# Retention + SwiGLU kernel: the ramp written in a new order, with powers of the decay spread by TensorE, small operations moved to GpSimd, and loads issued at other places

## The chip, the cores and the metric

One core of a Trainium2 chip (trn2) runs the kernel. The metric is the time of one execution in microseconds (us), the median of the runs. TensorE (PE, with its weight loads PEld), VectorE (DVE), ScalarE (ACT), GpSimd (POOL) and SyncE (SP, which issues loads) each run their own instruction list in order and wait for one another by semaphores.

## What is computed

Decayed linear attention in blocks (4 sequences of 768, 8 heads of width 64), whose output goes row by row through an RMS norm and a gated feed-forward layer (512 to 1536 to 512):

```python
Dmask = np.where(rel >= 0, lam[:, None, None] ** rel[None, :, :], 0.0)
intra = np.einsum('bhic,bhjc->bhij', qb, kb) * Dmask[None]
intra = np.einsum('bhij,bhjd->bhid', intra, vb)
inter = np.einsum('bhid,bhde->bhie', qb * lam_pow[None], kv_state)
kv_state = lam_block[None, :, None, None] * kv_state + np.einsum('bhsd,bhse->bhde', kb_dec, vb)
...
xn = x / rms * rms_g
g = xn @ w_gate
silu = g * (1.0 / (1.0 + np.exp(-g)))
return (silu * (xn @ w_val) @ w_out)
```

## The kernel before

The 3072 rows are cut into six row blocks m of 512, the heads into four pairs p, the hidden width into twelve blocks f of 128. `Pair(m, p)` makes the attention of a row block and a pair, `Weights(f)` turns the raw weights of block f into f16 high and low parts, `Hidden(m, f)` makes the gate and value products (three parts each: high by high, low by high, high by low), `Norm(m)` the RMS norm. In the names of the ramp p03 is `Pair(0, 3)`, w2 is `Weights(2)`, h0 is `Hidden(0, 0)`, n0 is `Norm(0)`.

The first six units of row block 0, the attention of row blocks 0 and 1 and the weights of blocks 0 to 5 are issued by `ramp()`, one list of calls written out by hand. Nothing reorders them: each call puts its instructions at the end of the lists of its engines, and each engine works through its list in order. After the ramp `unit()` runs the remaining units, one after the other.

A Pair on TensorE: `scores` (tile pa, 8 products), `state_sums` (pst, 6 or 8 products of 64 columns), `mix_chunks` (po, 8 products), `mix_states` (po again, 6 products). On the other engines: `decay_k` on ScalarE, `decay_a` on VectorE (pa times the mask), `decay_q`, `states` on VectorE, `keep_output` and `keep_squares`. `row_sums` (pss, 4 products per pair), `mean`, `root` (y, on GpSimd), `spread` (pr) and `scaled` (xn), `high`, `low` make the normed rows that the gate products read, in four parts kk.

A Weights block: `lift` (ScalarE), `convert` (VectorE, two operations, whole or by parts), `square` (ScalarE), `norm` (pn, TensorE), `scale`, `high` (ScalarE), `low`, `undo`; its part for the output product has `lift_o`, `convert_o`, `high_o`, `low_o`.

The products share few banks: `pg` and `pv` hold one gate and one value product each, and in turn the state sums and the mixed output of pairs that are not `odd`; the next user waits until the last reader is done. The other banks are po0 to po3 and `ps`.

Loads: `load_next()` issues the next of a fixed list on the SP queue. Here q11 stands for the load of q, k and v of `Pair(1, 1)` (two pieces of 512 KB), g3 for the gate and value weights of block 3 (`raw_gv`, 1024 KB) and o3 for its output weights (`raw_o`, 512 KB). The list is q10, g1 with o0, g2 with o1, q11, g3, q12, g4, q13, g5 and so on; o2, o3 and later ones are issued at the end of `convert_o` of the block two below. A load into a buffer that is still read waits on SP, and what is behind it waits as well.

`busy(n)` issues n products whose result nobody reads.

Of the kernel before, what the change touches and what calls it, by code (L numbers as in the profile page):

```python
# [23 lines left out]
def retention_swiglu_kernel(  # L24
# [130 lines left out]
    def powers(p, part):  # L155
        if part < 2:
            h = 2 * p + part
            nc.vector.tensor_tensor_scan(
                mask[:, h, :], lam_b[:, h : h + 1].broadcast_to([P, P]), ident, 0.0,
                ALU.mult, ALU.add,  # L160
            )
        else:
            nc.vector.tensor_tensor_scan(
                pw[:, p, :], lam_p[:, p : p + 1].broadcast_to([P, P]), zeros, 1.0,
                ALU.mult, ALU.add,
            )
# [23 lines left out]
    def scales_of(pmax):  # L190
        nc.vector.tensor_reduce(gmax, pmax[:, :P], axis=mybir.AxisListType.X, op=ALU.max)
        nc.vector.tensor_single_scalar(ge, gmax.bitcast(I32), 0x7F800000, op=ALU.bitwise_and)
        nc.vector.tensor_scalar_min(ge, ge, float(252 * EXP))
        nc.vector.tensor_scalar(sx.bitcast(I32), ge, -1.0, float(253 * EXP), ALU.mult, ALU.add)
        nc.vector.tensor_scalar(gs, gcol, sx, XS, ALU.mult, ALU.mult)
        nc.vector.tensor_scalar_add(cx.bitcast(I32), ge, float(EXP))
        nc.vector.tensor_scalar_mul(cx, cx, 1.0 / (XS * WS))
# [15 lines left out]

    zeros = wg[:, NF - 1, 1].bitcast(F32)[:, :P]
    nc.scalar.mul(zeros, ones, 0.0)
# [142 lines left out]
    class Weights:  # L358
# [79 lines left out]
        def undo(self):  # L438
            inv = small.tile([P, 2], F32, tag="inv", name=f"inv_{self.f}")
            nc.vector.tensor_scalar_add(inv.bitcast(I32), self.e2, float(64 * EXP))  # L440
            nc.vector.tensor_scalar_mul(cg[:, self.f, :], inv, cx)
# [19 lines left out]
    class Pair:  # L461
# [48 lines left out]
        def states(self):  # L510
            m, p = self.m, self.p
            for c in range(GC):
# [4 lines left out]
                if g % SEQ_CH == 0:  # L517
                    nc.vector.tensor_copy(new, self.pst[:, c, :])
                else:
# [298 lines left out]
    def ramp():  # L818
# [5 lines left out]
        powers(0, 0)  # L824
        largest()
        powers(0, 1)
        powers(2, 0)
        busy(2, 3)
        powers(2, 1)
        busy(4)  # L830
        powers(1, 2)
        powers(3, 1)
        powers(1, 0)
        powers(1, 1)
        p00.decay_k()
# [72 lines left out]
        n0.spread()
        w0.scale()
        w1.convert(1)  # L910
        w0.high(0)
        w1.square(1)
        n0.scaled(0)
        n0.high(0)
        p10.state_sums()
        busy(2, 1)
# [3 lines left out]
        n0.scaled(1)  # L920
        w0.high(1)
        n0.high(1)
        p10.states()
        n0.scaled(2)
        n0.high(2)
        p10.mix_chunks()
        load_next()
        n0.scaled(3)
        busy(2, 3)
        n0.low(1, nc.vector)  # L930
        w0.low(0)
        n0.low(2, nc.vector)
        n0.high(3)
        n0.low(3, nc.vector)
        w0.lift_o()
        w1.high(0)
        w0.low(1)
        w0.undo()
        w1.low(0)
        busy(2, 3)  # L940
        w1.pn = ps_att.tile([P, 2, G], F32, tag="ps", name="pn_1")[:, 0]
        w1.norm(slice(1, 2))
        w1.scale(slice(1, 2))
        p10.decay_q(nc.gpsimd)
        p10.mix_states()
        p10.keep_output(nc.scalar)
        h0.gate(0)
        h0.val(0)
        h0.gate(1)
        n0.low(0, nc.gpsimd)  # L950
        h0.gate(2)
        h0.val(1)
        h0.val(2)
        w2.lift()
        h0.silu()
        w2.convert(part=0)
        h1.gate(0)
        w1.undo()
        h0.mul()
        h1.gate(1)  # L960
        w3.lift()
        w1.high(1)
        h1.gate(2)
        w2.convert(part=1)
        w1.low(1)
        w2.square(0)
        w2.square(1)
        h1.val(0)
        h1.val(1)
        w3.convert(part=0)  # L970
        w0.convert_o()
        p10.keep_squares()
        h1.silu()
        w2.pn = ps_att.tile([P, 2, G], F32, tag="ps", name="pn_2")[:, 0]
        w2.norm()
        load_next()
        w2.scale()
        w2.high(0)
        p11.decay_k()
        w2.high(1)  # L980
        h1.val(2)
        p11.scores()
        h2.gate(0)
        w3.convert(part=1)
        w2.low(0)
        high_o(0)
        w2.undo()
        h1.mul()
        h2.gate(1)
        w1.lift_o()  # L990
        w2.low(1)
        h2.gate(2)
        h2.val(0)
        h2.val(1)
        h2.val(2)
        w3.square(0)
        h0.high()
        w1.convert_o()
        h0.low()
        low_o(0, nc.vector)  # L1000
        h0.out(3)
        p11.decay_a()
        high_o(1)
        h2.silu()
        h2.mul()
        w3.square(1)
        load_next()
        p12.decay_k()
        h0.out(2)
        p11.decay_q(nc.vector)  # L1010
# [3 lines left out]
        w2.lift_o()  # L1014
        h1.high()
        p11.state_sums()
        p11.states()
        w2.convert_o()
        w3.high(1)
        w3.high(0)  # L1020
        p11.mix_chunks()
        w4.lift()
        load_next()
        w3.low(0)
        w3.low(1)
        p12.scores()
        p11.mix_states()
        h3.gate(0)
        high_o(2)
        w3.undo()  # L1030
        w4.convert(part=0)
        h3.gate(1)
        h0.out(0)
        h1.low()
        h3.gate(2)
        p12.decay_q(nc.vector)
        w4.convert(part=1)
        p11.keep_squares()
        p11.keep_output(nc.scalar)
        low_o(1, nc.gpsimd)  # L1040
        h3.val(0)
        h1.out(2)
        h3.val(1)
        p12.decay_a()
        w3.lift_o()
        h3.val(2)
        h3.silu()
        h0.out(1)
        w4.square(0)
        w4.square(1)  # L1050
        w4.pn = ps_att.tile([P, 2, G], F32, tag="ps", name="pn_4")[:, 0]
        w4.norm()
        p11.add_squares(nc.vector)
        h3.mul()
        w4.scale()
        p12.state_sums()
        p12.states()
        p12.mix_chunks()
        p12.mix_states()
        w4.high(1)  # L1060
        load_next()
        w4.high(0)
        w4.lift_o()
        low_o(2, nc.vector)
        w4.low(1)
        w4.low(0)
        p12.keep_output(nc.vector)
        p12.keep_squares()
        w5.lift()
        p13.scores()  # L1070
        h4.gate(0)
        h1.out(0)
        p13.decay_q(nc.gpsimd)
        h2.high()
        p13.decay_k()
        w3.convert_o()
        high_o(3)
        load_next()
        h4.gate(1)
        w5.convert(part=0)  # L1080
        h1.out(1)
        h4.gate(2)
        load_next()
        w4.undo()
        h2.low()
        w5.convert(part=1)
        w5.square(0)
        h4.silu()
        h4.val(0)
        h4.val(1)  # L1090
        h4.val(2)
        h1.out(3)
        h2.out(1)
        p13.decay_a()
        low_o(3, nc.vector)
        w5.square(1)
# [244 lines left out]
```

## Time and profile before

| | us |
|---|---|
| median of 3 runs | 676.25 (675.94 to 676.49) |
| the profiled execution, whole | 677.75 |
| its span, first to last instruction | 675.9 |
| TensorE busy in the span | 667.7 |

The profile is of one execution. Its span leaves out 1.85 us of the execution's own time (677.75 less 675.9). In the trace the ramp ends at 95.25 us, where the gate product of the first `unit()` starts.

### The profile page before, as it was taken

To read this page: it belongs to the slowest core of one execution; us is meant where nothing else is said; L and a number is where in the kernel's file an instruction comes from. 1 tells how busy PE (TensorE), PEld (TensorE's weight loads), DVE (VectorE), ACT (ScalarE), POOL (GpSimd) and SP (SyncE) were. 2 spreads that over 40 slices of the span, in tenths; PEclk is the share of its full clock that TensorE was granted. 3 is DMA by queue.
4 is the path that set the end of the run, shared out by engine and by line. 5 is a ranking of instruction groups with operands and counts; after the bars stand their busy time and mean duration, and the time that the engine had idled before them with its cause. 6 is when DMAs were issued, how large, how long until landed. Compare 5 with 4: busy or idle time off the path is not lost.

```text
span 675.9 us, 9923 instructions
## 1 busy us (share of the span) xinstructions
PE 667.7 (99%) x4156; PEld 359.1 (53%) x4156; DVE 323.1 (48%) x575; ACT 248.3 (37%) x438; POOL 78.8 (12%) x76
## 2 busy tenths in 40 slices
PE   8998999999999999999999999999999999999997
PEld 7856665555666444554444555444465444444443
DVE  7797857777545386332812322631341462211112
ACT  3785556776425435322213222221331221211111
POOL 2200130011214303230000111000011000000000
PEclk9999999999999999999999999999999999999999
DMA  8936622541014201122001022100100000100001
GB/s 320 365 120 225 233 109 97 185 156 63 1 64 171 79 0 63 64 99 89 1 0 58 29 102 79 47 0 1 63 1 1 1 0 1 63 0 1 1 0 62
DMA packets 14299, 50.96 MB, mean 75 GB/s; under 512 B 1712, under 2 KB 1968, under 8 KB 12848
## 3 DMA queue, kind: packets, MB, share of 16 engines
q1 hardware_dynamic: 13968, 49.69, 20.2%
q8 instruction: 32, 0.52, 0.3%
q10 hardware_dynamic: 288, 0.66, 0.3%
q14 instruction: 11, 0.09, 0.0%
HBM read 44.05 MB, written 6.29 MB: 74 GB/s over the span
## 4 chain that ended last, share of the span: by engine, by line
PE 95%; DMA 2%; DVE 2%; issue 0%; ACT 0%; DVEq 0%; SPq 0%
PE pv L697 27%; PE pg L697 27%; PE acc L716 10%; PE acc L718 9%; PE acc L717 9%; PE pa L476 4%; PE po L536 3%; PE po L547 3%; PE pst L505 2%; DMA raw_gv<-in_weights_dram 1%; PE pss L600 1%; DMA cs<-in_consts_dram 0%; DVE xn L675 0%; DVE w L233 0%; PE pss L647 0%
## 5 line engine op out<-in xcount | busy, mean ns | idle before, releaser
L697 PE MATMUL pv<-x,wv 128*128 128x512 f16 x864 | 199.1, 379 | 1.9 <-ACT x L567 1.9
L697 PE MATMUL pg<-x,wg 128*128 128x512 f16 x864 | 199.9, 379 | 0.2 <-ACT x L680 0.2
L789 DVE SCALAR_TENSOR_TENSOR sg<-pv,cv,sg 128x512 f32<-128x512 f32 x54 | 40.5, 750 | 241.7 <-PE pv L697 241.7
L697 PEld LDWEIGHTS <-wv 128*128 128x128 f16 x864 | 84.3, 98 | 102.7 <-issue 3.2
L697 PEld LDWEIGHTS <-wg 128*128 128x128 f16 x864 | 82.7, 98 | 101.2 <-issue 4.9
L718 PE MATMUL acc<-wo,hh 128*128 128x512 f16 (+1 forms) x288 | 110.3, 383 | 0.0
L717 PE MATMUL acc<-wo,hh 128*128 128x512 f16 (+1 forms) x288 | 110.2, 383 | 0.0
L782 ACT ACTIVATE sg<-pg,cg 128x512 f32<-128x512 f32 x72 | 49.3, 684 | 163.4 <-PE pg L697 163.3
L799 ACT CAST hh<-sg 128x512 f16<-128x512 f32 (+1 forms) x72 | 44.5, 617 | 162.1 <-DVE sg L789 158.3
L716 PE MATMUL acc<-wo,hh 128*128 128x512 f16 x216 | 82.0, 380 | 0.0
L496 POOL TENSOR_TENSOR qkv<-qkv,pw 128x512 f32<-128x512 f32 x22 | 28.2, 1285 | 239.7 <-PE pa L476 233.9
L806 DVE TENSOR_TENSOR hh<-sg,hh 128x512 f16<-128x512 f32 x54 | 38.0, 704 | 27.4 <-ACT hh L799 27.4
L716 PEld LDWEIGHTS <-hh 128*128 128x128 f16 x216 | 21.1, 98 | 26.6 <-issue 2.8
L718 PEld LDWEIGHTS <-hh 128*128 128x128 f16 x216 | 21.1, 98 | 25.5
L717 PEld LDWEIGHTS <-hh 128*128 128x128 f16 x216 | 21.2, 98 | 23.4
L716 PE MATMUL acc<-wo,hl 128*128 128x512 f32 x72 | 32.4, 450 | 0.0
L492 DVE TENSOR_TENSOR a<-pa,mask 128x1024 f32<-128x1024 f32 x24 | 29.3, 1222 | 5.9 <-PE pa L476 5.9
L476 PE MATMUL pa<-qkv 64*128 64x128 f32 x384 | 27.9, 285 | 0.0
L476 PEld LDWEIGHTS pa<-qkv 64*128 64x128 f32 x384 | 23.3, 187 | 8.3 <-issue 6.5
L536 PE MATMUL po<-a,qkv 128*64 128x128 f32 x384 | 25.7, 275 | 0.0
L486 ACT ACTIVATE qkv<-qkv,mask 128x256 f32<-128x256 f32 x48 | 21.7, 502 | 8.8 <-DMA qkv<-in_qkv_dram 8.8
L567 ACT COPY x<-po 128x512 f32<-128x512 f32 x22 | 12.8, 580 | 28.6 <-PE po L547 28.6
(131 smaller groups left out, 598.0 us busy)
## 6 DMA issues: line engine op xcount, KB each, us to landing
qkv<-in_qkv_dram SPq DMA_DIRECT2D x47, 512.0 KB, 4.8
raw_gv<-in_weights_dram SPq DMA_DIRECT2D x11, 1024.0 KB, 7.0
raw_o<-in_weights_dram SPq DMA_DIRECT2D x12, 512.0 KB, 3.8
out_dram<-o SPq DMA_DIRECT2D x23, 256.0 KB, 2.3
partial<-in_weights_dram SPq DMA_DIRECT2D x2, 512.0 KB, 12.3
qkv<-in_qkv_dram ACTq DMA_DIRECT2D x1, 512.0 KB, 4.1
out_dram<-o SPq DMA_DIRECT2D x1, 128.0 KB, 2.1
out_dram<-o ACTq DMA_DIRECT2D x1, 128.0 KB, 1.9
```

The costliest lines, as they stand in the source:

```text
L476: nc.tensor.matmul(self.pa[:, j, c, :], self.kT[r, c, :], self.qT[r, c, :], start=True, stop=True,)
L492: nc.vector.tensor_mul(self.a, self.pa, decay.broadcast_to([P, 2, GC, P]))
L496: eng.tensor_mul(self.qT, self.qT, pw[:, p : p + 1, :].broadcast_to([P, GC, P]))
L536: nc.tensor.matmul(po[r, c, :], self.v[:, c, r], self.a[:, j, c, :], start=c == 0, stop=False, skip_group_check=True,)
L697: nc.tensor.matmul(ps, w[:, kk, :], x[:, kk, :], start=i == kk == 0, stop=i == 2 and kk == NK - 1,)
L716: nc.tensor.matmul(acc, hl[:, ts_], oh, start=first, stop=False)
L717: nc.tensor.matmul(acc, hh[:, ts_], ol, start=False, stop=False)
L718: nc.tensor.matmul(acc, hh[:, ts_], oh, start=False, stop=last)
L782: nc.scalar.activation(self.sg, self.pg, AF.Silu, scale=cg[:, self.f, 0:1])
L789: nc.vector.scalar_tensor_tensor(out, self.pv, factor, self.sg, ALU.mult, ALU.mult)
L799: nc.scalar.copy(self.hh, self.sg)
L806: nc.vector.tensor_sub(self.hl, self.sg, hh)
```

## The change

- The powers of lam that multiply q (`pw`) were four scans on VectorE. Now the mask's first row is spread by two products a pair (`spread_powers`, tile pp in bank po3) and multiplied by lam on ScalarE (`powers_of`). The operation that made a tile of zeros for the scans is gone.
- `scales_of` is cut: the largest value is taken on VectorE early, the five small operations that follow run on GpSimd. `undo` runs on GpSimd for w0, w1, w3 and w5. `low_o` of blocks 0 to 3 is on GpSimd (before: block 1 alone of these), of blocks 4 and 5 on VectorE.
- The first state of a sequence (`first_state`) is a call of its own, on ScalarE for most pairs.
- One group of unread products is put in bank po0, that of the state sums: `busy(3, 0)`.
- The ramp's list is written in another order throughout. q10, g1 and g2, q11 are issued behind one `mix_states` each.

```diff
+    def powers(h):
+        nc.vector.tensor_tensor_scan(
+            mask[:, h, :], lam_b[:, h : h + 1].broadcast_to([P, P]), ident, 0.0,
+            ALU.mult, ALU.add,
+        )
+
+    def spread_powers(p):
+
+        ps = ps_out.tile([P, DM], F32, tag="po3", name=f"pp_{p}")
+        for j, r in enumerate(heads):
+            nc.tensor.matmul(
+                ps[r, :P], ident[:, 0:1].broadcast_to([P, D]), mask[:, 2 * p + j, :], start=True, stop=True
             )
...
+        return ps
+
+    def powers_of(p, ps):
+        nc.scalar.mul(pw[:, p, :], ps[:, :P], lam_p[:, p : p + 1])
...
+    def scales_of(eng):
+        eng.tensor_scalar_min(ge, ge, float(252 * EXP))
+        eng.tensor_scalar(sx.bitcast(I32), ge, -1.0, float(253 * EXP), ALU.mult, ALU.add)
+        eng.tensor_scalar(gs, gcol, sx, XS, ALU.mult, ALU.mult)
+        eng.tensor_scalar_add(cx.bitcast(I32), ge, float(EXP))
+        eng.tensor_scalar_mul(cx, cx, 1.0 / (XS * WS))
...
-    zeros = wg[:, NF - 1, 1].bitcast(F32)[:, :P]
-    nc.scalar.mul(zeros, ones, 0.0)
...
-        def undo(self):
+        def undo(self, eng=nc.vector):
             inv = small.tile([P, 2], F32, tag="inv", name=f"inv_{self.f}")
...
+        def first_state(self, eng=nc.vector):
             m, p = self.m, self.p
+            for c in range(GC):
+                g = m * GC + c
+                if g % SEQ_CH == 0:
+                    copy = nc.scalar.copy if eng is nc.scalar else eng.tensor_copy
+                    copy(state[:, p, g % SLOTS, :], self.pst[:, c, :])
```

The ramp's list around the first gate products and around the loads, as it stands now:

```python
row_sums(0, 3)
busy(2, 3)
w0.pn = ps_out.tile([P, DM], F32, tag="po3", name="pn_0")
w0.norm(slice(0, 1))
...
busy(3, 0)
w0.norm(slice(1, 2))
...
n0.spread()
w1.convert(0)
p10.scores()
w0.scale(slice(1, 2))
n0.scaled(3)
p10.state_sums()
w1.square(0)
n0.scaled(2)
...
n0.scaled(0)
...
n0.scaled(1)
n0.high(1)
p10.decay_a()
...
h0.gate(0)
n0.low(2, nc.gpsimd)
w0.high(1)
p10.mix_chunks()
w1.lift_o()
w0.lift_o()
p10.first_state(nc.scalar)
w1.lift(1)
...
w2.lift()
h0.val(0)
n0.low(1, nc.vector)
w1.high(0)
w2.convert(part=0)
h0.gate(1)
h0.gate(2)
h0.silu()
w1.convert(1)
load_next()
w2.convert(part=1)
load_next()
busy(4)
h1.gate(0)
...
h0.val(1)
...
w0.convert_o()
```

**TensorE around the first gate product (tile pg).** Before, all of `Pair(1, 0)` (pa, pst, then po twice) and four groups of unread products stand ahead of it (pn is the norm of w0 and w1, pr the norm's spread):

```order
L476 MATMUL pa_0_410<-qkv_0_267 128x128 x8
L146 MATMUL unread_421<-ident 128x128 x2
L412 MATMUL pn_424<-ssq_397,ones 128x2
L633 MATMUL pr_433<-ident,y_408 128x128 x4
L505 MATMUL pst_0_450<-qkv_0_267 64x64 x6
L146 MATMUL unread_457<-ident 128x128 x2
L412 MATMUL pn_424<-ssq_430,ones 128x1
L536 MATMUL po_0_475<-a_0_419,qkv_0_267 64x128 x8
L146 MATMUL unread_488<-ident 128x128 x2
L146 MATMUL unread_503<-ident 128x128 x2
L412 MATMUL pn_506<-ssq_430,ones 128x1
L547 MATMUL po_0_475<-qkv_0_267,state 64x128 x6
```

Now only pa and pst of `Pair(1, 0)` stand ahead of it, and po of `Pair(1, 0)` comes behind:

```order
L146 MATMUL unread_414<-ident 128x128 x2
L416 MATMUL pn_417<-ssq_395,ones 128x1
L146 MATMUL unread_423<-ident 128x128 x3
L416 MATMUL pn_417<-ssq_395,ones 128x1
L645 MATMUL pr_438<-ident,y_431 128x128 x4
L480 MATMUL pa_0_445<-qkv_0_273 128x128 x8
L509 MATMUL pst_0_458<-qkv_0_273 64x64 x6
L416 MATMUL pn_417<-ssq_465,ones 128x1
L709 LDWEIGHTS wg
L709 MATMUL pg_0_489<-x_276,wg 128x512
```

Both po rows of `Pair(1, 0)` moved behind the first gate product; of eight unread products five are left ahead of it, and four more now stand ahead of the first gate product of h1; pn of w0 is cut in two.

**SP, the loads from q11 on.** Before (q11, g3, o2, q12, o3, g4, o4):

```order
L86 DMA qkv_1_389<-in_qkv_dram 128x1024 x2
L101 DMA raw_gv_484<-in_weights_dram 128x2048
L109 DMA raw_o_590<-in_weights_dram 128x1024
L86 DMA qkv_2_598<-in_qkv_dram 128x1024 x2
L109 DMA raw_o_665<-in_weights_dram 128x1024
L101 DMA raw_gv_683<-in_weights_dram 128x2048
L109 DMA raw_o_713<-in_weights_dram 128x1024
```

Now (q11, g3, q12, o2, o3, g4, q13):

```order
L86 DMA qkv_1_388<-in_qkv_dram 128x1024 x2
L101 DMA raw_gv_534<-in_weights_dram 128x2048
L86 DMA qkv_2_537<-in_qkv_dram 128x1024 x2
L109 DMA raw_o_572<-in_weights_dram 128x1024
L109 DMA raw_o_638<-in_weights_dram 128x1024
L101 DMA raw_gv_642<-in_weights_dram 128x2048
L86 DMA qkv_3_670<-in_qkv_dram 128x1024 x2
```

o2 moved behind q12, and q13 ahead of o4.

**ScalarE around the silu of h2 (tile sg_2).** Before, o1 is lifted (L221, raw_o_387) ahead of it; w3 is lifted further up:

```order
L430 ACTIVATE wg<-w_546,sc_602 128x512
L486 ACTIVATE qkv_1_389<-qkv_1_389,mask 128x4x64 x2
L430 ACTIVATE wv<-w_546,sc_602 128x512
L249 CAST wo_629<-wg 128x512
L221 ACTIVATE wg<-raw_o_387 128x512
L408 ACTIVATE junk_0_659,ssq_658<-w_564 128x512
L799 CAST hh_0_661<-sg_0_548 128x512
L249 CAST wo_676<-wg 128x512
L782 ACTIVATE sg_2_678<-pg_2_622,cg 128x512
L408 ACTIVATE junk_1_681,ssq_658<-w_564 128x512
```

Now w3 is lifted (L225, w_628) and then o2 (L225, raw_o_572) ahead of it:

```order
L794 ACTIVATE sg_1_606<-pg_1_545,cg 128x512
L811 CAST hh_0_626<-sg_0_530 128x512
L225 ACTIVATE w_628<-raw_gv_534 128x1024
L225 ACTIVATE wg<-raw_o_572 128x512
L434 ACTIVATE wv<-w_512,sc_589 128x512
L794 ACTIVATE sg_2_634<-pg_2_612,cg 128x512
L253 CAST wo_644<-wg 128x512
L412 ACTIVATE junk_0_682,ssq_681<-w_628 128x512
L412 ACTIVATE junk_1_685,ssq_681<-w_628 128x512
```

The instruction that needs o2 moved ahead of the silu of h2 and of both squares of w3 (L412, junk).

## Rows read from the trace of the kernel before

**Rows 1.** The page, part 1: busy us, share of the span, instructions.

```profile
PE 667.7 (99%) x4156; PEld 359.1 (53%) x4156; DVE 323.1 (48%) x575; ACT 248.3 (37%) x438; POOL 78.8 (12%) x76
```

**Rows 2.** Windows by stage: busy time per engine, TensorE clock, DMA share, GB/s.

```profile
22.00:24.25 2.25, 2.25 (x21) 2.13 (x20) 0.79 (x2) 1.91 (x6) 0.00 (x0) 1.00 1.04 390
32.48:57.90 25.42, 25.23 (x171) 14.08 (x170) 21.94 (x46) 18.49 (x35) 1.61 (x1) 1.00 0.52 178
57.90:60.00 2.10, 0.19 (x2) 0.00 (x1) 1.50 (x3) 2.10 (x5) 0.00 (x0) 1.00 0.96 326
60.00:95.25 35.25, 35.25 (x239) 24.27 (x238) 27.35 (x49) 21.02 (x39) 8.33 (x7) 1.00 0.49 193
```

**Rows 3.** Timeline at 57.9 us: start, microseconds, engine, line; in brackets idle before.

```profile
47.97 0.43 SPq L101 DMA_DIRECT2D raw_gv<-in_weights_dram  x1
...
57.34 1.12 ACT L221 ACTIVATE w<-raw_gv 128x1024 f32<-128x1024 f32 x1 [4.16 <-DMA raw_gv<-in_weights_dram]
...
59.99 1.02 PE L697 MATMUL pv<-x,wv 128*128 128x512 f16 x4 [1.91 <-ACT x L567]
```

**Rows 4.** Timeline of TensorE in the ramp.

```profile
1.46 2.93 PE L146 MATMUL unread<-ident 128*128 128x128 f32 x12 [1.46 <-POOL one L210]
...
6.53 1.38 PE L146 MATMUL unread<-ident 128*128 128x128 f32 x10
...
9.55 1.09 PE L536 MATMUL po<-a,qkv 128*64 128x128 f32 x16
...
12.11 1.16 PE L476 MATMUL pa<-qkv 64*128 64x128 f32 x16
...
38.03 2.75 PE L697 MATMUL pg<-x,wg 128*128 128x512 f16 x12
```

**Rows 5.** Timeline of the norm of row block 0, in four engines.

```profile
24.36 0.16 DVE L620 TENSOR_SCALAR ms<-pss 128x4 f32<-128x4 f32 x1 [1.57 <-PE pss L600]
...
24.67 1.03 POOL L624 TENSOR_TENSOR y<-ms,power 128x4 f32<-128x4 f32 x1 [6.23 <-DVE ms L620]
...
26.42 1.14 PE L633 MATMUL pr<-ident,y 128*128 128x128 f32 x8
...
30.00 0.60 ACT L680 CAST x<-xn 128x512 f16<-128x512 f32 x1
...
31.40 1.40 DVE L675 SCALAR_TENSOR_TENSOR xn<-x,gs,pr 128x512 f32<-128x512 f32 x2
```

**Rows 6.** Timeline, single instructions of ScalarE and VectorE.

```profile
28.58 0.69 DVE L233 SCALAR_TENSOR_TENSOR w<-raw_gv,w 128x512 int32<-128x512 int32 x1
...
28.67 0.71 ACT L430 ACTIVATE wg<-w,sc 128x512 f16<-128x512 f32 x1
...
33.35 0.68 ACT L221 ACTIVATE wg<-raw_o 128x512 f32<-128x512 f32 x1
...
36.01 1.15 ACT L221 ACTIVATE w<-raw_gv 128x1024 f32<-128x1024 f32 x1 [0.90 <-ACT x L567]
...
37.06 0.67 ACT L782 ACTIVATE sg<-pg,cg 128x512 f32<-128x512 f32 x1
37.19 0.69 DVE L230 TENSOR_SCALAR w<-w 128x1024 int32<-128x1024 int32 x1
```

**Rows 7.** Timeline of the load queue (SP): issues.

```profile
29.34 0.33 SPq L101 DMA_DIRECT2D raw_gv<-in_weights_dram  x1
...
42.58 0.33 SPq L109 DMA_DIRECT2D raw_o<-in_weights_dram  x1
```

**Rows 8.** DMA view, loads issued at 29.34, 42.58, 47.97, 47.60: KB, us to landing.

```profile
raw_gv<-in_weights_dram SPq DMA_DIRECT2D x1, 1024.0 KB, 5.4
raw_o<-in_weights_dram SPq DMA_DIRECT2D x1, 512.0 KB, 3.6
raw_gv<-in_weights_dram SPq DMA_DIRECT2D x1, 1024.0 KB, 9.3
raw_o<-in_weights_dram SPq DMA_DIRECT2D x1, 512.0 KB, 5.5
```

More of the change, by code (lines that the diff above doesn't have):

```diff
@@ L941, in ramp @@
+        h0.val(1)
+        w1.square(1)
+        h0.val(2)
         w1.pn = ps_att.tile([P, 2, G], F32, tag="ps", name="pn_1")[:, 0]
         w1.norm(slice(1, 2))
[L943 to L956, printed above, removed]
@@ new lines, in ramp @@
+        h0.mul()
+        w1.high(1)
+        w2.scale()
+        h1.val(0)
+        w1.low(1)
+        p10.decay_q(nc.gpsimd)
+        w2.high(0)
+        w2.undo(nc.vector)
+        w1.undo(nc.gpsimd)
+        h1.silu()
+        h1.val(1)
+        h2.gate(0)
+        w2.low(0)
+        h2.gate(1)
+        h2.gate(2)
+        h0.high()
+        w3.lift()
+        p10.states(True)
+        w2.lift_o()
+        w2.high(1)
+        h2.silu()
+        w1.convert_o()
+        w3.convert(part=0)
+        w3.convert(part=1)
@@ L1013, in ramp @@
         w3.scale()
-        w2.lift_o()
-        h1.high()
[L1016 to L1020, printed above, removed]
+        h0.out(0)
+        p11.states(True)
+        w3.undo(nc.gpsimd)
+        w3.high(0)
+        h2.val(1)
+        w4.lift()
+        w2.convert_o()
+        w3.low(0)
+        h3.gate(0)
+        h0.out(3)
+        w4.convert(part=0)
+        p11.decay_q(nc.vector)
+        w3.high(1)
+        h1.high()
+        p12.decay_k()
@@ L1025, in ramp @@
+        p12.first_state(nc.vector)
+        w4.pn = ps_att.tile([P, 2, G], F32, tag="ps", name="pn_4")[:, 0]
+        w4.norm()
         w3.low(1)
[L1026 to L1035, printed above, removed]
-        p12.decay_q(nc.vector)
[L1037 to L1040, printed above, removed]
+        h0.out(2)
@@ L1041, in ramp @@
+        w4.scale()
+        w4.undo(nc.vector)
+        w4.high(0)
+        p11.keep_output(nc.scalar)
+        h0.out(1)
+        h1.out(0)
+        p11.keep_squares()
+        p12.states(True)
+        w4.low(0)
+        w3.convert_o()
+        p12.decay_q(nc.vector)
+        w5.lift()
+        h2.high()
+        h4.gate(0)
+        w4.high(1)
+        h4.gate(1)
+        p13.decay_k()
+        w4.lift_o()
         h3.val(0)
         h1.out(2)
+        high_o(2)
+        h2.low()
+        w5.convert(part=0)
@@ L1043, in ramp @@
+        w5.convert(part=1)
+        load_next()
+        high_o(3)
         h3.val(1)
-        p12.decay_a()
-        w3.lift_o()
         h3.val(2)
[L1047 to L1053, printed above, removed]
+        w5.square(0)
+        w5.square(1)
+        p13.scores()
         h3.mul()
-        w4.scale()
-        p12.state_sums()
-        p12.states()
+        low_o(2, nc.gpsimd)
@@ L1076, in ramp @@
[L1076 to L1081, printed above, removed]
-        h4.gate(2)
[L1083 to L1087, printed above, removed]
+        p12.keep_output(nc.scalar)
+        p13.decay_q(nc.vector)
+        w4.convert_o()
+        w5.lift_o()
+        w5.pn = ps_att.tile([P, 2, G], F32, tag="ps", name="pn_5")[:, 0]
+        w5.norm()
+        w5.scale()
+        h4.gate(2)
```

411 lines of the change are left out of this document (191 added, 220 removed).

## Prediction

> **What bounds the kernel now.** I read the page first: TensorE is busy for 667.7 of 675.9 us [rows 1], so all idle time of the engine that is the limit comes to 8.2 us, and no change of the other engines can give more than a part of that. The ramp is the first 95.25 us, and the change touches nothing behind it. The windows by stage show where TensorE stands still in it: from the first gate product at 32.48 to 57.9 it is busy for 25.23 of 25.42 us, then for 0.19 of 2.10, then without a gap until the ramp ends at 95.25 [rows 2]. So behind 32.5 us one wait of 1.9 us is all there is. Its timeline names the cause: TensorE wants bank pv for a value product of h3, pv is freed by a copy on ScalarE, and ScalarE stood for 4.16 us at the lift of w4, whose load g4 was issued at 47.97 and came at 57.3 [rows 3]. TensorE's granted clock is 1.00, which is the 2.4 GHz level, in every one of these windows, in the one with the wait too [rows 2]: an idle stretch of 2 us cost no clock here.
>
> Ahead of 32.5 us TensorE is mostly busy, but some of it is unread work. What matters there is when the first gate product has all its inputs. So the prediction needs two things: when h0 is through in the new order, and which waits the rest then meets.
>
> **The change, part by part. First part, up to the row sums.** Before, the scores of pair 2 start at 12.11 [rows 4] and the row sums are done at 24.3, as the mean begins at 24.36 [rows 5]. TensorE works on nearly without a gap between, so this stretch is priced in products. Ahead of pair 2 the first group has one more unread product; 12 passes, six products, took 2.93 and end at 4.39, while the scores of pair 0 end at 6.53, where the next unread group starts [rows 4]; the scores take 1.16 and the product between them about 0.5, so 0.4 to 0.5 were idle and the seventh product, also 0.5, fits there: 0. The second group falls from 5 to 2; five took 1.38 [rows 4], 0.28 each, so -0.8. `spread_powers` adds eight products like those of po, 8 for 1.09 [rows 4], 0.14 each: +1.1. Sum +0.3: row sums done at 24.6 (between 24.3, if the spreads hide in small gaps, and 25.1, if the removed products give nothing).
>
> The four scans that go leave VectorE idle where TensorE is the limit: 0. `powers_of` and the states' copies on ScalarE have no row of their shape; a 128x512 cast takes 0.60 [rows 5] and they are smaller, so between 0 and 0.6 each; I take 0.3, and TensorE has pairs' products to do meanwhile. The small operations on GpSimd have none either. The nearest is the power on 128x4, 1.03 [rows 5], so 0 to 1.03 each: five end by about 19.5 at the latest if they start at 14, and what they give is first read by xn at 27.4; the decay of q3 behind them then ends by 21, when its products come up. Two of them in `undo` end at most 2.1 us after `scale`, about when the silu that reads them is due. 0 at both ends. `busy(3, 0)` waits for VectorE's last read of p03's sums, near 21 us, and stands at 25: 0.
>
> **Second part, the norm and h0.** The mean takes 0.16 and starts at 24.7, y follows 0.15 later with 1.03 and the spread with 1.14 [rows 5]: 27.3. Now VectorE makes all four xn in a row, two of them 1.40 [rows 5], in the order 3, 2, 0, 1: they end at 28.1, 28.8, 29.5, 30.2. A cast follows each, 0.60 [rows 5]; the gate product reads part 0 first (30.2) and part 1 last (30.9). Four products of a gate are a third of 2.75 [rows 4], 0.9, so it ends at 31.6.
>
> From there TensorE has po of p10 (1.1) and three parts of h0 (2.7): 35.4. But h1's first gate part needs bank pg, that is h0's silu, and ScalarE's list from 30.9 has w0.high(1) (0.71), two `lift_o` (0.68 each), a state copy (0.3), half a lift (0.68), w2's whole lift (1.15) and w1.high(0) (0.71) [rows 6]: 35.8, and with the silu, 0.67 [rows 6], 36.5. The four unread products (1.1) fill just this gap, so they cost nothing, and taking them out would give nothing. Then h1.gate(0) ends at 37.4 and the rest of h0's value product (1.8) at 39.2. The states' products of p10 (six, 0.8) are still to do. Before, the same work, p10 whole, was done at 38.03 + 0.9 = 38.9 [rows 4]. The new order is here at 39.2 + 0.8 = 40.0: **1.1 us later**.
>
> **Third part, the rest of the ramp.** Before, it took 95.25 - 38.9 = 56.35, of which 1.9 were the wait; 54.4 is work, and TensorE's work is the same now but for one pn (0.2). Without any wait the ramp would end at 40.0 + 54.4 + 0.2 = 94.6. Now the waits, by walking the lists on with the same prices.
>
> *The load g3* goes out when w1.convert(1) is done. It stands on VectorE behind w2's lift, which ends at 35.1 (the ScalarE sum above), one operation of 0.69 and one convert of a half, at most 1.4 and I take 1.1 [rows 6]: 36.9. Before it went out at 29.34 [rows 7]; "early" is not true of this one. It took 5.4 [rows 8], so 42.4. q12 follows, 1.05 MB, which at the 390 GB/s that the queue reaches when full [rows 2] is 2.7: 45.1; then o2, 0.52 MB: 46.4. ScalarE is at the lift of o2 at 44.8 (silu of h1 to 43.0, a cast 0.6, w3's lift 1.15). It waits 1.6 us there, and the silu of h2 and both squares of w3 are behind. At 46.4 come lift 0.68, high 0.71, silu 0.67, a cast 0.6, two squares of about 0.8: 50.2 to 50.7. TensorE is at the norm of w3 at 50.1. Wait 0.1 to 0.6; I take 0.3. Before, o2 went out at 42.58 into an empty queue and took 3.6 [rows 8]; with 3.6 there would be no wait. But o3, with pieces of q12 still in front, took 5.5 and g4 behind it 9.3 [rows 8], so I go by the bytes in front.
>
> The Trainium skill ("DMA: Bandwidth & Descriptors", section "Queues, rings and completion order") says that on each DMA engine a queue's descriptors are consumed in ring order. By that o2 cannot land ahead of g3 and q12, as in my sum; by the 3.6 us of the empty queue the ramp would end 0.3 earlier. The 5.5 of o3 agrees with the page [rows 8].
>
> *The load g4*, the old wait: it goes out when w3 is converted, 44.8 + 1.9 or so, 46.8 against 47.97 [rows 3]. It lands at 52.2 with 5.4, at 56.1 with 9.3. ScalarE reaches w4's lift at 51.9; the silu of h3 ends 4.6 after that lift starts (lift 1.15, high 0.71, cast 0.6, two small ones 0.9, cast 0.6, silu 0.67), and TensorE wants pg for the sums of p12 at about 57.4. So any landing up to 52.8 is free and each us beyond costs one. With 5.4 to 6 us: 0 to 0.2, I take 0.2. The old place of the wait, pv for h3's value product, is now far behind the copy that frees it.
>
> *A pn* of w2 shares its bank with pn of w1 and waits for w1.scale: 0.3 by the walk.
>
> Sum: 94.6 + 0.3 + 0.2 + 0.3 = 95.4 against 95.25: **+0.15 us** on the span of 675.9. The rest of the program is the same list, without gaps. On the median of 676.25 that is 676.4. What the measurement of this kernel can tell from no change is about 0.2%, 1.35 us.
>
> **The rivals.** *Slower: g4 comes late again.* If it takes the 9.3 us it took before, it lands at 56.1, ScalarE stands from 51.9 on, and TensorE waits 3.3 at the state sums of p12: 676.25 + 0.15 - 0.2 + 3.3 = 679.5. It turns the verdict when the landing is later than about 54.2, 7.4 us after the issue. For it: three loads, g3, q12 and o2, stand closer in front of it than before; against: the queue has drained by then by the bytes. Chance, with o2 a us later counted in: 0.27.
>
> *Faster: no waits, and the first product earlier.* The end at 94.6 alone gives -0.65, 675.6, still within the bound. It takes 0.7 more: the row sums at 24.3, the first bound above, and 0.4 out of ScalarE's list, whose instructions follow each other some 0.1 closer than their lengths (36.01 + 1.15 = 37.16, the next starts at 37.06 [rows 6]); then the unread products are the limit. 674.9. For it: the old wait of 1.9 is really gone; against: TensorE's floor of work leaves nothing else to win. Chance 0.21.
>
> *No effect beyond trading:* the forecast. The wait of 1.9 goes, 1.1 is lost ahead of h1 and 0.8 in new waits. Chance 0.52, from 675.0 to 677.6. The range for 8 in 10 takes in most of both rivals: 674.7 to 679.0.
>
> **What the profile after would show.** Right: row sums done near 24.6; xn in one row on VectorE from 27.4; the first gate product near 30 with TensorE idle for over a us before it; an unread group just ahead of h1's first gate part near 36.5; g3 issued near 37; ScalarE waiting near 45 at L225 for o2; the ramp's end near 95.4. Wrong: a wait of over a us between 45 and 60 us on TensorE (the first rival, if behind the silu of h3), or the row sums before 24, or h1's first gate part before 36 (the second).

## The result, and the profile after

The changed kernel takes **679.23 us** (678.74 to 680.0), the kernel before 676.25 on the same chip: ratio 1.004, 95% interval 1.0025 to 1.0055. It is slower by 3.0 us, more than twice the 1.35 us that the prediction took as the bound of no change. The forecast was 676.4 and "same"; the measured time lies 0.2 above the range. The profiled execution of the changed kernel took 680.0, 0.8 above its median. Three executions that took far longer than all others (991.7 in a2, 3963.69 in a5, 2302.37 of the kernel before) are left out of the medians below.

The page's first part, against [rows 1]: TensorE is busy 1.7 us longer, and the span is 678.1 against 675.9.

```profile
PE 669.4 (99%) x4172; PEld 359.8 (53%) x4172; DVE 318.8 (47%) x557; ACT 250.3 (37%) x447; POOL 81.8 (12%) x89
```

The ramp now ends at 97.50, where before it ended at 95.25 [rows 2]. Behind it both profiles have the same 580.6 us left (678.1 less 97.50; 675.9 less 95.25), so all of the change lies in the ramp. The timeline of the norm and h0, which answers to [rows 4, 5]:

```profile
25.01 0.16 DVE L632 TENSOR_SCALAR ms<-pss 128x4 f32<-128x4 f32 x1 [1.56 <-PE pss L612]
...
26.68 1.14 PE L645 MATMUL pr<-ident,y 128*128 128x128 f32 x8
...
27.12 0.42 DVE L234 TENSOR_SCALAR w<-w 128x512 int32<-128x512 int32 x1
...
27.57 0.69 DVE L237 SCALAR_TENSOR_TENSOR w<-raw_gv,w 128x512 int32<-128x512 int32 x1
...
28.47 2.72 DVE L687 SCALAR_TENSOR_TENSOR xn<-x,gs,pr 128x512 f32<-128x512 f32 x4
...
31.24 0.38 PE L709 MATMUL pg<-x,wg 128*128 128x512 f16 x1 [1.52 <-ACT x L692]
...
31.90 0.81 PE L709 MATMUL pg<-x,wg 128*128 128x512 f16 x3 [0.28 <-ACT x L692]
...
32.18 1.30 POOL L500 TENSOR_TENSOR qkv<-qkv,pw 128x512 f32<-128x512 f32 x1
...
32.50 1.52 DVE L438 SCALAR_TENSOR_TENSOR wg<-w,sc,wg 128x512 f16<-128x512 f32 x1
...
36.84 0.69 ACT L794 ACTIVATE sg<-pg,cg 128x512 f32<-128x512 f32 x1 [0.37 <-PE pg L709]
...
37.58 1.02 PE L709 MATMUL pg<-x,wg 128*128 128x512 f16 x4
37.71 0.33 SPq L101 DMA_DIRECT2D raw_gv<-in_weights_dram  x1
```

The mean starts at 25.01 (24.36 in [rows 5]). The spread ends at 27.82, but VectorE is at the convert of w1 (L234, L237) until 28.26, and the first xn starts at 28.47, not at 27.4. TensorE stands for 1.52 us ahead of the first gate product and 0.28 within it. In the windows from the mean to the first gate product it is idle for 0.33 of 8.18 us before, and for 1.67 of 6.24 now. Before:

```profile
24.30:32.48 8.18, 7.85 (x87) 6.63 (x86) 7.00 (x17) 6.04 (x13) 3.43 (x3) 1.00 0.96 367
```

Now:

```profile
25.00:31.24 6.24, 4.57 (x53) 4.03 (x53) 4.45 (x12) 4.65 (x10) 2.87 (x5) 1.00 0.90 360
```

At 32.50 a low of w0 takes VectorE 1.52 us, while GpSimd runs a decay of q (L500); its like takes 0.74 at 33.94. The timeline of o2 and what waits behind it:

```profile
38.85 0.80 SPq L86 DMA_DIRECT2D qkv<-in_qkv_dram  x2
...
40.53 4.76 SPq L109 DMA_DIRECT2D raw_o<-in_weights_dram  x2
...
48.26 0.67 ACT L225 ACTIVATE wg<-raw_o 128x512 f32<-128x512 f32 x1 [3.51 <-DMA raw_o<-in_weights_dram]
...
49.44 0.67 ACT L794 ACTIVATE sg<-pg,cg 128x512 f32<-128x512 f32 x1
...
50.16 0.57 PE L509 MATMUL pst<-qkv 128*64 128x64 f32 x12 [0.76 <-ACT sg L794]
...
52.05 0.38 PE L416 MATMUL pn<-ssq,ones 128*128 128x2 f32 x2 [0.35 <-ACT junk L412]
```

q12 goes out at 38.85 and o2 at 40.53 (the row holds o2 and o3). ScalarE stands for 3.51 us at the lift of o2 (L225), which comes at 48.2; the silu of h2 follows at 49.44, and TensorE waits 0.76 for its bank at the state sums of p11 and 0.35 at the norm of w3. The load g4, which made the old wait [rows 3], is in time: w4's lift starts without a wait.

```profile
53.50 1.15 ACT L225 ACTIVATE w<-raw_gv 128x1024 f32<-128x1024 f32 x1
```

### The profile page after: what moved, and what is told of

Its sections match the earlier page's. It is cut to its first block, busy times and chain, and to the rows that moved or that the text cites. A ratio compares the mean times of both kernels' runs of the same rounds, so it can differ in the third digit from the quotient of the medians.

```text
span 678.1 us, 9960 instructions
## 1 busy us (share of the span) xinstructions
PE 669.4 (99%) x4172; PEld 359.8 (53%) x4172; DVE 318.8 (47%) x557; ACT 250.3 (37%) x447; POOL 81.8 (12%) x89
## 4 chain that ended last, share of the span: by engine, by line
PE 97%; DVE 2%; ACT 1%; issue 0%; POOL 0%; DVEq 0%; POOLq 0%; ACTq 0%
PE pg L709 27%; PE pv L709 27%; PE acc L728 10%; PE acc L730 9%; PE acc L729 9%; PE pa L480 4%; PE po L548 3%; PE po L559 3%; PE pst L509 2%; PE unread L146 1%; PE pss L612 1%; DVE xn L687 0%; PE pn L416 0%; PE pss L659 0%; DVE wg L438 0%; ACT junk L412 0%
## 5 line engine op out<-in xcount | busy, mean ns | idle before, releaser
L500 POOL TENSOR_TENSOR qkv<-qkv,pw 128x512 f32<-128x512 f32 x20 | 25.7, 1286 | 222.5 <-PE pa L480 210.0
L818 DVE TENSOR_TENSOR hh<-sg,hh 128x512 f16<-128x512 f32 x54 | 38.0, 704 | 27.4 <-ACT hh L811 27.4
```

Source lines behind the costliest of these rows:

```text
L500: eng.tensor_mul(self.qT, self.qT, pw[:, p : p + 1, :].broadcast_to([P, GC, P]))
L818: nc.vector.tensor_sub(self.hl, self.sg, hh)
```

## The experiments

Each time is a median beside the kernel before on the same chip, which took 676.3 to 676.4 in the three comparisons. Single executions differ, so I also read from each profile when the mean of the norm starts, when the ramp ends, and what lies between.

| profile | mean starts | ramp ends | between | median us | ratio, 95% interval |
|---|---|---|---|---|---|
| before | 24.36 | 95.25 | 70.9 | 676.25 | |
| before again | 25.88 | 94.97 | 69.1 | | |
| b1, w4's lift later | 24.12 | 92.93 | 68.8 | 675.78 | 0.999 (0.9982 to 0.9999) |
| b2, spreads alone | 27.58 | 96.60 | 69.0 | 678.27 | 1.0032 (1.0021 to 1.0043) |
| b3, small operations alone | 24.53 | 93.61 | 69.1 | 676.04 | 1.000 (0.9988 to 1.0013) |
| after | 25.01 | 97.50 | 72.5 | 679.23 | 1.004 (1.0025 to 1.0055) |
| a1, o2 ahead of q12 | 24.54 | 95.82 | 71.3 | 679.75 | 1.0047 (1.003 to 1.0064) |
| a2, lift of o2 later | 24.95 | 95.97 | 71.0 | 678.97 | 1.004 (1.0026 to 1.0053) |
| a3, no unread products | 25.13 | 98.53 | 73.4 | 679.3 | 1.0042 (1.0027 to 1.0058) |
| a4, xn first | 24.23 | 100.73 | 76.5 | 683.99 | 1.0104 (1.0086 to 1.0122) |
| a5, gap filled, wrong bank | 25.06 | 98.14 | 73.1 | 679.36 | 1.0049 (1.0035 to 1.0063) |
| a6, p10 early | 25.17 | 98.35 | 73.2 | 680.51 | 1.0063 (1.0044 to 1.0083) |
| a7, p10 early, lift later | 24.04 | 96.79 | 72.8 | 679.11 | 1.0038 (1.0025 to 1.0052) |
| a9, gap filled, free bank | 24.75 | 96.70 | 72.0 | 678.76 | 1.0034 (1.0022 to 1.0046) |

### The old wait: before again, and b1

> The kernel before, unchanged: a second profile of it. The profiled execution of before took 677.75, its runs without the wait of the profile's own have a median of 676.25 and, in the last comparison, spans of about 674.4 against 675.9 in the profile. New theory: the wait of 1.9 us for g4 is in that one profile but not in most executions, so the changed kernel had nothing to gain there. Then this profile shows g4 landed before ScalarE reaches its lift, no gap of TensorE near 58, and a ramp that ends near 93.5 with a span of 674 to 674.8. Rival, the prediction's reading: the wait is in every execution and the 1.5 us lie elsewhere: gap near 58 of 1.5 to 2 us again, ramp end above 94.8.

The kernel before, profiled a second time, on g4:

```profile
49.50 0.43 SPq L101 DMA_DIRECT2D raw_gv<-in_weights_dram  x1
...
57.03 1.15 ACT L221 ACTIVATE w<-raw_gv 128x1024 f32<-128x1024 f32 x1 [2.34 <-DMA raw_gv<-in_weights_dram]
...
59.71 0.59 PE L697 MATMUL pv<-x,wv 128*128 128x512 f16 x2
```

Issued at 49.50, it lands at 57.0, 7.5 us later instead of 9.3 [rows 8]; ScalarE waits 2.34 us and TensorE not at all: its value product of h3 at 59.71 has no wait. The theory's numbers failed all the same: the ramp ended at 94.97, because the mean of the norm began 1.5 us later than in the first profile. Both profiled executions (677.75 and 677.5) lie over a us above the median, for two different reasons.

> The kernel before, with ScalarE's lift of w4 moved behind the copy of p11's output that frees the bank which TensorE waited for. If the wait of 1.9 us for g4 is in most executions, the median falls by 1.5 to 1.9: 674.5 against 676.3 on the same chip. If it is in the profile alone, the median stays within 0.5: 676.3.

```diff
         w3.high(0)
         p11.mix_chunks()
-        w4.lift()
         load_next()
...
         p11.mix_states()
+        p11.keep_squares()
+        p11.keep_output(nc.scalar)
+        w4.lift()
         h3.gate(0)
```

675.78 against 676.32: the median falls by 0.5, or by 0.7 if taken from the ratio (0.1 to 1.2 by its interval), and not by 1.9. I take 0.6. The wait is in some executions, and its size follows from how long g4 takes to land, not from how early the ramp is: in b3 below, g4 goes out at 47.97 just as in the first profile, but lands 7.7 us later instead of 9.3, and TensorE waits 0.30 us instead of 1.91. Why the load took 9.3 us in the first profile stays open.

### Parts of the change in the kernel before: b2 and b3

> The kernel before with only the first part of the change: the four scans for pw replaced by spread_powers and powers_of, the largest value read early, the second group of unread products cut from five to two. The prediction's sum for the row sums was +0.3 by the products; the changed kernel showed +0.65. My theory: the list costs what its products do, +0.1 to +0.4 at the row sums, and the rest of the ramp follows it: 676.3 + 0.3 = 676.6. Rival, the spreads' products with their waits on VectorE's scans and on bank po3 are the main cost of the change: +1.5 or more, 677.8.

```diff
         pm = scales()
+        largest_of_all(pm)
         p00.scores()
-        powers(0, 2)
+        busy(2, 3)
+        p00.decay_a()
+        powers_of(0, spread_powers(0))
         p00.decay_q(nc.gpsimd)
-        busy(5)
-        p00.decay_a()
...
-        powers(2, 2)
+        powers_of(2, spread_powers(2))
```

(p1 and p3 likewise.) The rival won: +1.9 us (678.27 against 676.32), of which the trace shows 1.7 at the mean (27.58 against 25.88 in the second profile of before, whose first products ran as slowly). TensorE's row sums there wait for a square on ScalarE, behind the `powers_of`:

```profile
19.03 1.16 PE L606 MATMUL pss<-ones,sq 128*128 128x128 f32 x8 [0.65 <-ACT sq L584]
```

In the old order this part of the change costs much more than its products. The new order hides them better: its mean starts at 24.95 in the median of nine profiles, near the 24.6 of the products' sum.

> The kernel before with only the small operations of the change on GpSimd: the five after the largest value, and undo of w0, w1, w3 and w5. The prediction's claim: they change nothing, 676.3 within 0.4. Rival: GpSimd's decays of q or the lows stand behind them and come later: 676.8 or more.

```diff
-        scales_of(pm)
+        largest_of_all(pm)
+        scales_of(nc.gpsimd)
...
-        w0.undo()
+        w0.undo(nc.gpsimd)
```

Ratio 1.000: as claimed. This profile again has a short wait for pv behind g4, the third size of it after 1.91 and none:

```profile
47.97 0.43 SPq L101 DMA_DIRECT2D raw_gv<-in_weights_dram  x1
...
55.68 1.14 ACT L223 ACTIVATE w<-raw_gv 128x1024 f32<-128x1024 f32 x1 [2.52 <-DMA raw_gv<-in_weights_dram]
...
58.35 1.02 PE L699 MATMUL pv<-x,wv 128*128 128x512 f16 x4 [0.30 <-ACT x L569]
```

### The load o2: a1 and a2

> The changed kernel, with the load q12 issued behind o2 instead of ahead of it. My theory: ScalarE's 3.51 us at the lift of o2 is the load's place in the queue; o2 was issued at 40.53 behind g3 and q12 and landed at 48.2. With q12 behind it, o2 should land near 44.6 and ScalarE should wait less than 0.5 us; TensorE's two waits behind it, 0.76 at the state sums of p11 and 0.35 at the norm of w3, go: 679.2 - 1.1 = 678.1, at the most 1.85 less (the same two waits on its weight loads): 677.4. Rival, the place in ScalarE's list alone costs it and TensorE is held by something else: wait gone in the trace, time 679.2.

```diff
         w2.convert(part=1)
-        load_next()
         busy(4)
...
         w0.convert_o()
+        load_next()
         w1.scale(slice(1, 2))
```

Timeline of the loads and of ScalarE:

```profile
40.06 0.33 SPq L109 DMA_DIRECT2D raw_o<-in_weights_dram  x1
...
44.17 0.67 ACT L225 ACTIVATE wg<-raw_o 128x512 f32<-128x512 f32 x1
...
46.21 0.69 ACT L794 ACTIVATE sg<-pg,cg 128x512 f32<-128x512 f32 x1 [0.75 <-PE pg L709]
...
53.44 1.14 ACT L225 ACTIVATE w<-raw_gv 128x1024 f32<-128x1024 f32 x1 [1.77 <-DMA raw_gv<-in_weights_dram]
```

Issued at 40.06, o2 is there when ScalarE comes to it at 44.17, 4.1 us later instead of 7.7. The silu of h2 now waits for TensorE and not the reverse. So the wait was the queue's. The Trainium skill ("DMA: Bandwidth & Descriptors", section "Queues, rings and completion order") says that on each DMA engine a queue's descriptors are consumed in ring order; the trace agrees, with 7.7 us behind q12 and at most 4.1 ahead of it.

> The changed kernel, loads as they are, with the lift of o2 moved on ScalarE behind the silu of h2 and both squares of w3. My theory: the wait for o2 costs only by what stands behind it, the silu of h2 and the squares; then o2 may land at 48.2 and TensorE loses neither 0.76 nor 0.35: 678.1, the same as with o2 ahead of q12. Rival, the load matters elsewhere too (the lift and the convert of o2 are late for the first products of block 2's output): between 678.1 and 679.2 here, and less with o2 ahead of q12.

```diff
         p10.states(True)
-        w2.lift_o()
         w2.high(1)
...
         w3.square(1)
+        w2.lift_o()
         h2.val(0)
```

```profile
46.62 0.69 ACT L794 ACTIVATE sg<-pg,cg 128x512 f32<-128x512 f32 x1 [1.32 <-PE pg L709]
...
49.10 0.66 ACT L225 ACTIVATE wg<-raw_o 128x512 f32<-128x512 f32 x1
...
49.27 0.57 PE L509 MATMUL pst<-qkv 128*64 128x64 f32 x12
```

The silu of h2 at 46.62 instead of 49.44, and the state sums without a wait. From the mean to the ramp's end the two take 71.3 and 71.0 us against 72.5: the wait for o2 costs 1.2 to 1.5 in the trace. But the medians, 679.75 and 678.97, hardly differ from 679.23. For a2 the clock is a likely reason. In six of a2's nine runs the mean granted clock was 0.999 or 1.000, with spans of 676.0 to 676.8; in three it was 0.997 or 0.998, with 678.3 to 679.1, 2.1 more. The changed kernel's four runs at 1.000 had spans of 676.7 to 678.1. So a2 gains about 0.9 where the clock holds. For a1 the clock does not explain it: its four runs at 0.996 or 0.997 had spans of 677.4 to 677.8, between those of its other two, 676.4 and 678.1. What o2 is worth is thus read from the traces; neither median shows it.

### Where the clock falls: a3, a5 and a9

> The changed kernel without the four unread products ahead of the first gate product of h1. The prediction's claim: they fill a gap that the silu of h0 leaves, so taking them out gives nothing: h1's first gate product stays at 37.58 (the silu ends at 37.53) and the time at 679.2, within 0.4. Rival: they stand on the path, as 1.05 us of TensorE's work: 678.2.

```diff
-        busy(4)
         h1.gate(0)
```

Time unchanged, as the prediction claimed: 679.3 against 679.23. But its profile fell into the lower clock (windows of 2 us; the third number from the end is the granted clock), and TensorE's timeline shows the price:

```profile
28.00:30.00 2.00, 1.84 (x30) 1.58 (x31) 1.97 (x6) 1.42 (x4) 0.54 (x2) 1.00 1.04 414
30.00:32.00 2.00, 0.59 (x1) 0.10 (x1) 2.00 (x4) 1.89 (x4) 1.92 (x2) 0.82 0.22 86
32.00:34.00 2.00, 1.98 (x9) 0.87 (x10) 1.97 (x4) 2.00 (x5) 1.59 (x2) 0.50 0.00 0
34.00:36.00 2.00, 2.00 (x19) 1.35 (x16) 2.00 (x4) 1.54 (x3) 0.00 (x0) 0.82 0.00 0
```

```profile
31.36 2.10 PE L709 MATMUL pg<-x,wg 128*128 128x512 f16 x4 [1.52 <-ACT x L692]
...
37.90 0.69 ACT L794 ACTIVATE sg<-pg,cg 128x512 f32<-128x512 f32 x1 [1.31 <-PE pg L709]
...
38.64 1.02 PE L709 MATMUL pg<-x,wg 128*128 128x512 f16 x4 [0.84 <-ACT sg L794]
```

TensorE stands for 1.52 us ahead of the first gate product, from about 31.4 on the granted clock is 0.50, the lower of its two levels, and the four products take 2.10, where the changed kernel's went from 31.24 to 32.71, 1.47, with a gap of 0.28 among them. How much a fall costs differs: a3's four runs at 0.997 had spans 0.6 longer in the mean than its three at 0.999 or 1.000.

> The changed kernel, with five unread products (1.4 us) in the 1.52 us that TensorE stood idle ahead of the first gate product. In one of the experiments the granted clock fell to 0.50 from about 31.4 on, just behind such an idle stretch, for some 3.4 us, and the four first products took 2.10 instead of 1.2. Theory: in a part of the executions that idle stretch costs the clock, about 1.7 us each time; with the stretch filled the granted clock is 1.0 in every run and the median falls by 0.5 to 1.2: 678.0 to 678.7. Rival: the clock falls in few executions and the products that nobody reads gain nothing: 679.2 or, if they delay the first gate product, 0.2 more.

```diff
         w1.scale(slice(0, 1))
+        busy(5)
         h0.gate(0)
```

```profile
31.39 2.48 PE L146 MATMUL unread<-ident 128*128 128x128 f32 x10 [1.62 <-DVE xn L687]
```

The edit missed its aim: the unread products stood in the bank of the norm's spread, waited 1.62 us for its reader xn, and then delayed the gate. The clock fell here as well.

> The changed kernel with five unread products ahead of the first gate product, now in a bank that nobody reads at that time (in the first try they stood in the bank of the norm's spread and waited for its readers). Theory: TensorE's idle stretch of 1.52 us is filled, the granted clock stays at 1.00 from 30 to 36 in the profile and is 0.999 to 1.0 in every run. The median: in the changed kernel one run in five had 0.997 with a span of 677.4 against 677.5, as the wait for o2 took up what the clock lost; so 679.2 or up to 0.3 less. Rival: the clock falls all the same (0.997 in some runs): then the idle stretch is not what it follows.

```diff
         w1.scale(slice(0, 1))
+        busy(5, 1)
         h0.gate(0)
```

```profile
30.98 0.38 PE L709 MATMUL pg<-x,wg 128*128 128x512 f16 x1 [0.30 <-ACT x L692]
```

With the stretch filled, TensorE waits 0.30, and all ten runs have a clock of 0.999 or 1.000. With the stretch of 1.52 us, 12 of the 27 runs of the changed kernel, a1, a2 and a3 had 0.996 to 0.998. The median is 678.76, 0.5 lower; the intervals overlap, so the size stays open.

### The way from the norm to h1: a4, a6 and a7

> The changed kernel, with VectorE's convert of w1 (and ScalarE's square of it) moved from ahead of the four xn to behind them. In the changed kernel the spread of the norm ended at 27.82 and the first xn began at 28.47, behind that convert. My theory: xn starts near 27.9, the first gate product 0.5 earlier, near 30.7, and the gain is kept: 678.7. Rival: ScalarE's list sets the silu of h0 and the gain is lost there: first gate product near 30.7 and 679.2. Second rival: the norm of w1 comes later by the convert and holds h1's first gate product: above 679.5.

```diff
-        w1.convert(0)
         p10.scores()
...
-        w1.square(0)
...
         n0.high(1)
+        w1.convert(0)
+        w1.square(0)
```

The first xn comes 2.95 us after the mean instead of 3.46, as expected, and then the second rival holds, one gate earlier than it was put: the norm of w1 stands ahead of h0's first gate product, not h1's, and TensorE waits 5.05 us for it. Timeline:

```profile
27.18 2.72 DVE L687 SCALAR_TENSOR_TENSOR xn<-x,gs,pr 128x512 f32<-128x512 f32 x4 [0.50 <-ACT wg L434]
...
28.66 2.27 POOL L695 TENSOR_TENSOR x<-xn,x 128x512 f16<-128x512 f32 x2 [1.44 <-ACT x L692]
29.81 1.39 DVE L234 TENSOR_SCALAR w<-w 128x512 int32<-128x512 int32 x1
30.89 1.44 POOL L500 TENSOR_TENSOR qkv<-qkv,pw 128x512 f32<-128x512 f32 x1
31.24 1.63 DVE L237 SCALAR_TENSOR_TENSOR w<-raw_gv,w 128x512 int32<-128x512 int32 x1
...
33.68 0.59 PE L416 MATMUL pn<-ssq,ones 128*128 128x1 f32 x2 [5.05 <-ACT junk L412]
```

The convert (L234, L237) takes 1.39 and 1.63 instead of 0.42 and 0.69: GpSimd runs two lows of the rows and a decay of q beside it.

> The changed kernel with the pair p10 put back into TensorE's idle stretches: its scores in place of the two unread groups in front of the norm's spread, its decay on VectorE in the wait for y, its first mixed products ahead of the first gate product, and w1's convert and norm behind that product. From the mean of the norm to the ramp's end the changed order takes 71.0 to 71.3 us without the wait for o2, the kernel before 68.8 to 69.1 without the wait for g4. Theory: 2.2 us of p10 (pa 1.16, po 1.09) stand on TensorE's path since the change, where before they stood in these stretches; but VectorE's lows of the rows bind next, so 0.7 comes back: 678.5 with the wait for o2 as it is. Rival, all of it comes back: 677.0. Second rival, the load o2, which goes out late all the same, takes the gain up: 679.2. The granted clock should be 1.0 in every run, as TensorE no longer stands still for over 1.4 us.

```diff
         row_sums(0, 3)
-        busy(2, 3)
+        p10.scores()
...
-        busy(3, 0)
...
         n0.root()
+        p10.decay_a()
...
         n0.high(1)
-        p10.decay_a()
-        w1.pn = w0.pn[:, 2:]
-        w1.norm(slice(0, 1))
-        w1.scale(slice(0, 1))
+        w1.convert(0)
+        p10.mix_chunks()
         h0.gate(0)
         n0.low(2, nc.gpsimd)
         w0.high(1)
-        p10.mix_chunks()
+        w1.square(0)
...
         n0.low(1, nc.vector)
+        w1.pn = w0.pn[:, 2:]
+        w1.norm(slice(0, 1))
+        w1.scale(slice(0, 1))
```

```profile
29.44 2.28 POOL L695 TENSOR_TENSOR x<-xn,x 128x512 f16<-128x512 f32 x2 [0.90 <-ACT x L692]
30.60 1.40 DVE L234 TENSOR_SCALAR w<-w 128x512 int32<-128x512 int32 x1
...
31.67 1.45 POOL L500 TENSOR_TENSOR qkv<-qkv,pw 128x512 f32<-128x512 f32 x1
...
32.04 1.64 DVE L237 SCALAR_TENSOR_TENSOR w<-raw_gv,w 128x512 int32<-128x512 int32 x1
...
33.71 0.63 ACT L412 ACTIVATE junk<-w 128x512 bf16<-128x512 f32 x1 [1.75 <-DVE w L237]
...
34.48 0.38 PE L416 MATMUL pn<-ssq,ones 128*128 128x1 f32 x2 [1.43 <-ACT junk L412]
```

My theory fell: 680.5, 1.3 slower. The products of p10 came forward, but the convert of w1 again ran beside GpSimd (1.40 and 1.64 us). ScalarE waited 1.75 for it, and TensorE 1.43, and the 1.59 ahead of the first gate product remained. One of the six runs had a clock of 0.997, which I had not expected either.

> The last one together with the lift of o2 behind the silu of h2 and the squares of w3. Without the wait for o2 what the early p10 gives is kept: the clean runs of the late lift alone had a span of 676.6 (678.4 as a time), so 677.7 with 0.7 back, 676.3 with all 2.2 back. If 677.7 or less, the order around the first gate product and the wait for o2 are together the greater part of what the change lost. Rival: still 678.4, then the loss behind the mean lies elsewhere, later than 50 us.

Both edits together: 679.11, from the mean to the ramp's end 72.8, with the clock at 0.50 for 3.4 us in this profile; its runs at 1.000 had spans of 676.6 to 678.3, against 676.0 to 676.8 for the late lift alone where the clock held. So the rival holds, and the two edits together are no better than the late lift alone.

## Why the prediction was wrong, point by point

**The step that failed first is "the wait of 1.9 goes".** The sum was made against the profiled execution's own time, whose 1.9 us were taken off in full. That execution took 677.75, 1.5 above the median, and I carried the difference over to the median without asking whether the wait was in it. It is worth 0.6 there (b1, 0.1 to 1.2). The forecast is too low by 1.3 for this alone.

**Row sums at 24.6.** They were done at 25.0; nine profiles with this head, or nearly, put the mean between 24.04 and 25.17, median 24.95. The size was about right, and a part of it wrong: the seventh unread product is not the matter, but the first products of p00 took 1.16 to 2.08 us by execution. Against the kernel before (24.12, 24.36, 24.53 and 25.88) the difference is some 0.5, within the scatter.

**Norm and h0, "1.1 us later".** Too small, for two reasons that the trace shows: the spread ended at 27.82 instead of 27.3, and VectorE was at the convert of w1 when it ended, an instruction of the list that I did not count. So xn came 1.1 late and the first gate product at 31.24 instead of 30.2. With at most 0.3 us of waits for loads the way from the mean to the ramp's end takes 71.0 to 71.3 us, against 68.8 to 69.1 before: +1.9 to 2.5, where the steps had 0.8 up to h1, 0.2 for the additional norm and 0.3 for the norm of w2, 1.3 in all. Most of it is TensorE's idle 1.52, 0.28 and 0.16 at the gate of h0: between the mean and the ramp's end it stands idle for 0.5 to 0.7 us in b0, b1 and b3, and for 2.1 and 2.3 in a2 and a1. The rest, 0.5 to 0.7, is more busy time, where the prediction had 0.2. That a better order could have it back is only argued: a4 and a6 tried, and met VectorE's slow convert.

**The load g3 "near 37":** 37.71. **o2 "lands at 46.4, wait 0.3":** the place and the mechanism were right, the size was not. It landed at 48.2, and TensorE lost 0.76 and 0.35; a1 and a2 put it at 1.2 to 1.5 in the trace.

**g4 free, the first rival's lateness:** free, as forecast, at most 6.6 us after its issue. That the rival's 679.5 lies near the measured time is chance: its wait did not come. The part of it that came true is "o2 a us later". **The unread products ahead of h1** cost nothing (a3), and **the small operations** nothing (b3); they take 0.19 to 0.30 each, one 0.59.

**"An idle stretch of 2 us cost no clock here"** was one profile. Elsewhere 1.5 us did in some executions: 2.1 us longer in a2, 0.6 in a3, nothing that shows in a1.

From the parts: +0.5 at the mean, +1.9 to 2.5 in the order, +0.7 to 1.5 for o2 (72.0 and 72.5 less 71.0 to 71.3), -0.6 for the old wait: 2.5 to 3.9, against 3.0 measured.

Open: how much of that order's loss is VectorE beside GpSimd. In the changed kernel itself one low lost 0.8 us so; moving that decay of q off GpSimd was not tried.

No version beat both kernels by more than the measurement tells; the nearest is the kernel before with w4's lift moved (b1, 0.9982 to 0.9999).

## What to carry to other kernels

A wait that one profile shows is not yet in the median: compare the profiled execution's time with the median first, and where it lies above, take a second profile or move the waiting instruction alone. Price each engine's list between two dependent steps from the order, not only the chain itself: one convert that stood ahead of xn, and one load ahead of o2, made a good part of the error beside the old wait. Work given to GpSimd is not free for VectorE beside it; look for which of VectorE's operations then stand on the path.

## What was not expected of the hardware

- Some of VectorE's operations take two to three times as long beside GpSimd: 0.42 became 1.40 (L234), 0.69 became 1.64 (L237), 0.74 became 1.52 (L438). Others do not: in the changed kernel four xn took 2.72 us, the last two of them beside the lows on GpSimd, and `decay_a` 1.22, as elsewhere. Those two read one input from a bank of TensorE's (pr, pa). The Trainium skill ("SBUF — State Buffer", section "Who interferes with whom") says that VectorE and GpSimd share one pair of ports of SBUF (the memory in which the tiles outside these banks lie) and that the one that comes second blocks until the other is through; but that an operation of VectorE with at most one input in SBUF, outside its modes that use two ports, does not contend. The traces agree, with 0.8 to 1.0 us of added time beside GpSimd operations of 1.1 to 1.5 us where both inputs lie in SBUF (L237, L438), and none for xn and `decay_a`; no run shows the mode of L234. The prediction did not weigh this.
- The first products of an execution run at little more than half speed until some time between 5 and 7.5 us, by execution (12 passes in 2.93 us, later 10 in 1.38 [rows 4]), while the granted clock reads 1.00 there: the same scores took 1.18 in the first profile of before and, in these two profiles of the changed kernel and of the one before, over 2 us:

```profile
5.16 2.06 PE L480 MATMUL pa<-qkv 64*128 64x128 f32 x16
```

```profile
5.42 2.08 PE L476 MATMUL pa<-qkv 64*128 64x128 f32 x16
```

- The granted clock fell to 0.50 for 3.4 us behind an idle stretch of TensorE of some 1.5 us, in some executions and not in others of the same kernel: by the mean clock in one of five of the changed kernel's runs, in none of ten with the stretch filled. Behind a stretch of 5.05 us (a4) it fell for 6.8, and all five runs had 0.995 or 0.996. One of the 57 runs of the kernel before in the three comparisons had 0.997 as well, so the stretch ahead of the first gate product is not its only place.
